# Two attention blocks in one kernel: B's diagonal key blocks packed in halves of 64 keys

## The chip, the cores and the metric

The kernel runs on one core of a Trainium2 chip. The time is device microseconds of one execution; of several executions the median is given. A core has five engines that run side by side, each with its own queue of instructions, worked off strictly in order: TensorE (PE in the profile; PEld is its weight loads), VectorE (DVE), ScalarE (ACT), GpSimd (POOL) and SyncE (SP, which here only issues transfers). They wait for each other through semaphores. Matmuls write into PSUM, here eight banks of 512 fp32 columns by 128 partitions; everything else lives in SBUF.

## The reference

Two independent attention blocks over 2048 rows of width 1024, 32 heads of 32, their outputs side by side.

```python
# A: plain attention over all 2048 keys
scores = jnp.einsum('bhqd,bhkd->bhqk', q, k) * Dh ** (-0.5)
p = _softmax(scores, axis=-1)
o = jnp.einsum('bhqk,bhkd->bhqd', p, v)          # then o @ wo
# B: four segments of 512 rows, causal inside a segment, with a running memory
for s in range(N):
    qs, ks, vs = (q[:, :, s].copy(), k[:, :, s].copy(), v[:, :, s].copy())
    logits = jnp.einsum('bhqd,bhkd->bhqk', qs, ks) * scale + mask   # mask: key after query
    p = _softmax(logits, axis=-1)
    a_dot = jnp.einsum('bhqk,bhkd->bhqd', p, vs)
    pq = phi(qs)
    num = jnp.einsum('bhld,bhde->bhle', pq, M)
    den = jnp.einsum('bhld,bhd->bhl', pq, z)[..., None] + 1e-06
    a_mem = num / den
    o = g * a_mem + (1.0 - g) * a_dot
    outs.append(o)
    pk = phi(ks)
    M = M + jnp.einsum('bhld,bhle->bhde', pk, vs)
    z = z + jnp.einsum('bhld->bhd', pk)
return o @ wo                                    # of the joined outs
```

## The kernel before

The program is not written out by hand: generator processes ask a planner (`Sched`, lines 172 to 370) for engines, banks and buffers, and the planner, while the kernel is built, simulates the engines with a cost for each operation and fixes the order of each queue. `Recorder` (lines 40 to 159) turns the data dependences of that order into semaphore waits, and `play` emits each engine's list. A dictionary `par` (line 398) holds the planner's settings: how far ahead of their use projections are due (`b`, `mem`, `ahead`), how many score slots must be left before PV work becomes urgent (`sl`, `pv`), at what rate B's units are mixed in among A's (`rate`) and so on.

Four heads make a group (128 partitions, 32 a head); each block has 8 groups. An **A unit** is one group by 256 queries (64 units); a **B unit** is one group in one segment of 512 queries and keys (32 units). For each the kernel works as follows.

Scores are computed transposed, keys on the partitions and queries on the columns. Four heads run side by side on the four row groups of TensorE (ROW mode), each writing its own bank. Six of the eight banks serve as three pairs for scores (`PAIRS`); banks 6 and 7 are shared by all other matmuls (`side`). `s_batch` (line 932) fills one step (u, k): for A, 256 queries against 256 keys for four heads, which takes two pairs; for B, k = 0 and 1 take two pairs, and k = 2 one pair. `parts` (line 914) lists what B's three steps hold, as (key tile, first query, width, first column): key tile 0 with all 512 queries; key tile 1 with the 384 from 128 on and, behind them, key tile 3 with its 128; key tile 2 with its 256. Each tile's first 128 columns are a diagonal block, half of which the causal mask throws away.

`exps` (line 988) turns a pair, 128x1024 scores, into probabilities: one exponential on ScalarE from PSUM to a slot of `PT` in SBUF (some of the first go to tiles not yet in use: WoB, OTA, OTB). For B, GpSimd then zeroes the masked triangle in place (`affine_select`, line 1011). The denominators need no maximum; a range check at the end raises a flag, and only if it is set a second, slower program runs (`shifted`, `emit` line 422).

`pv_unit` (line 1062) multiplies the probabilities by V and, for the denominators, by a block of ones, four heads on the four column groups (COL mode), into bank 6 or 7, and `finish` (line 1128) normalises on VectorE. A change between ROW and COL mode costs TensorE some time, so the planner runs COL work in stretches between score fills. COL work is also: projections (`proj`, line 685; `a_stream`, `b_proj`), the memory terms of B (`b_mem`, line 806; on VectorE it uses the buffer `mR` and, for the exponential of phi, a polynomial in `ze`, `ue`, `we` behind the lock `scr`), the output projections (`out_A`, `out_B`), and, where TensorE would be idle long, matmuls on zeros (`filler`).

At the end, every engine waits for the flag, loads it into a register and branches over the second program; SP then waits for all transfers (`drain`, line 143), channel by channel.

Of the kernel before, what the change touches and what calls it, by code (L numbers as in the profile page):

```python
# [39 lines left out]
class Recorder:  # L40
# [90 lines left out]
    def play(self, eng, name):  # L131
        for op in self.all:
            if op.ex != name:
                continue
            for d in op.waits:
                eng.wait_ge(self._sem_of(d), self.count[d])
            ins = op.fn(eng)
            if op.dma is not None:
                ins.then_inc(self.ch_sem[op.dma], 16)
            elif op.inc:  # L140
                ins.then_inc(self.sem[name], 1)

    def drain(self, eng):
        for c in range(self.NCH):
            if self.ch_n[c]:
                eng.wait_ge(self.ch_sem[c], 16 * self.ch_n[c])
# [226 lines left out]
def do(eng, fn, r=(), w=(), cost=0.1, prio=5, mode=None, tail=None, order=None, kb=None, hold=0.0, half=None):  # L373
    rq = Req()
    rq.half = half
    rq.order, rq.kb, rq.hold = order, kb, hold
    rq.eng, rq.fn, rq.r, rq.w, rq.cost, rq.prio, rq.mode = eng, fn, list(r), list(w), cost, prio, mode
    rq.tail = {"PE": 0.12, "ACT": 0.1, "DVE": 0.08, "POOL": 0.1, "SP": 2.0}[eng] if tail is None else tail
    return ("do", rq)
# [14 lines left out]
N256, N512 = 0.2235, 0.2175  # L394


class Kernel:
    par = dict(b=(16, 12, 9), mem=-4, memM=2, span=50, rate=0.58, ahead=20, sl=4, pv=10, ob=4, lead=6, b0=1, bpos=16, wob=40, mg=0.05, off=0, oks=(1,), sh=6, pd=4, o0=4, od=2, run=4, po=(1, 1), fp=2, fil=0.65, fs=0.15, ta=2, td=40, pvw=3, pvs=3, slk=0.12, pat=0.0, kh=3)
# [23 lines left out]
    def emit(self, block):  # L422
        def body(name):
            def f(eng):
                self.R.play(eng, name)
                self.R.after(eng, self.flagop)
                v = eng.value_load(self.flag[0:1, 0:1])
                with eng.If(v != 0):
# [4 lines left out]
                    if name == "SP":  # L433
                        self.R2.drain(eng)
                if name == "SP":
# [11 lines left out]
    def alloc(self):  # L447
# [16 lines left out]
        self.VB = [sb(f"VB{i}", [P, 4, 144]) for i in range(2)]  # L464
        self.PH = [sb(f"PH{i}", [P, 2, 512]) for i in range(2)]
# [8 lines left out]
        self.mR = sb("mR", [P, 512], F32)  # L474
# [13 lines left out]
        self.zero = sb("zero", [P, 32])  # L488
        self.maskbd = sb("maskbd", [P, P], F32)
        self.WoA = self.xA[:, :, :].rearrange("p i s -> p (i s)")[:, 0:NG * D].rearrange("p (j n) -> p j n", j=NG)  # L490
# [55 lines left out]
    def constants(self):  # L546
# [8 lines left out]
        for i in range(2):  # L555
            yield pool(lambda e, i=i: e.memset(self.VB[i][:, :, :], 1.0), [("VB", i)])
        yield pool(lambda e: e.memset(self.maskbd[:, :], 1.0), ["maskbd"])
# [124 lines left out]
    def pvprio(self):  # L682
        return 5 if len(self.slots.items) < self.par['sl'] or self.s_done else self.par['pv']
# [94 lines left out]
    def b_proj(self, n):  # L778
# [8 lines left out]
        for k in range(3):  # L787
# [7 lines left out]
            else:  # L795
                yield from self.proj(d, self.WB[k], ("WB", k), x, ["xB"], self.VT[n % 2][:, :], [("VT", n % 2)])
                yield self.turn(self.VB[b][:, :, 0:P], self.VT[n % 2][:, :], [("VT", n % 2)], [("VB", b)])
            if k == 1:
                Q.fire(("KQB", n))
            if k == 2:  # L800
                Q.fire(("VB", n))
            if n + 1 < 32:
                Q.spawn(self.load_WB(k, n + 1))
        Q.spawn(self.b_mem(n))

    def b_mem(self, n):
# [28 lines left out]
        if s > 0:  # L835
# [7 lines left out]
            def col(W, bank):  # L843
                def f(e):
                    for c in range(4):
# [5 lines left out]
            yield do("DVE", lambda e, bank=bank: e.transpose(self.mR[:, :], self.ps[:, bank, :]), r=[("ps", bank)], w=["mR"], cost=dve(512), prio=1)  # L851
            Q.give(self.side, [bank])
            yield do("DVE", lambda e: e.tensor_scalar(self.mr[:, :], self.mR[:, 0:512:32], 1e-6, None, ALU.add),
                     r=["mR"], w=["mr"], cost=0.1, prio=3)
            yield do("DVE", lambda e: e.reciprocal(self.mr[:, :], self.mr[:, :]), r=["mr"], w=["mr"], cost=0.2, prio=3)
            yield do("DVE", lambda e: e.transpose(self.mR[:, :].rearrange("p (a b) -> p a b", b=32), self.spread(self.mr[:, :])),
                     r=["mr"], w=["mR"], cost=dve(512), prio=3)
# [5 lines left out]
                     r=[("ps", bank), "mR", "gcol"], w=[("amem", b)], cost=dve(512) + 0.08, prio=1)  # L863
# [50 lines left out]
    def parts(self, u, k):  # L914
# [4 lines left out]
        return [[(0, 0, 512, 0)], [(1, 128, 384, 0), (3, 384, 128, 384)], [(2, 256, 256, 0)]][k]  # L919

    def s_all(self):
        Q = self.Q
        for u, k in self.order:
            yield from self.s_batch(u, k)
# [7 lines left out]
    def s_batch(self, u, k):  # L932
        Q = self.Q
        one = u[0] == "B" and k == 2
        parts = self.parts(u, k)
        if u[0] == "A":
            g = u[1]
            b = g % 2
            yield ("ev", ("KA", g, k))
            yield ("ev", ("QA", g, u[2]))  # L940
# [3 lines left out]
            keys = [("KA", b, k), ("QA", b, u[2])]  # L944
        else:
            b = u[1] % 2
            yield ("ev", ("KQB", u[1]))
            lhs = lambda t, hs: self.KQB[b][hs, 0, P * t:P * t + P]
            rhs = lambda q0, w, hs: self.KQB[b][hs, 1, q0:q0 + w]
            keys = [("KQB", b, 0), ("KQB", b, 1)]  # L950
        npair = 1 if one else 2
        slots = []
        for _ in range(npair):
# [4 lines left out]
        prs = yield acq(self.pairs, npair)  # L958
        mms = []
        if one:  # L960
            t, q0, w, _ = parts[0]
            for x in range(2):
                for h in (x, x + 2):
                    mms.append((prs[0][h // 2], x * 256, t, q0, w, h))
        else:
            for t, q0, w, col in parts:
                for h in range(4):
                    mms.append((prs[h // 2][h % 2], col, t, q0, w, h))

        def f(e, mms):  # L970
            for bk, col, t, q0, w, h in mms:
                hs = slice(32 * h, 32 * h + 32)
# [609 lines left out]
```

## Time and profile before

| what | us |
|---|---|
| median of 14 runs | 1115.26 (1113.3 to 1117.77) |
| the profiled execution | 1113.11 |
| its span | 1111.3 |
| TensorE matmuls (L973 scores, L1109 PV, L688 projections, L1197 and L1244 output) busy | 1044.9 |
| VectorE busy | 725.6 |
| GpSimd busy | 136.7, of it masks (L1011) 106.3 |
| granted TensorE clock, mean | 0.998 |

The profile is of one execution. A span begins with the first instruction and ends with the last. A busy time is the union of the instructions of an engine, so that overlapping ones count once; "mean ns of one" counts each from its own start to its own end, so in a closely packed queue the mean is longer than the distance from one to the next. A line number is that of the helper which recorded the instruction. "[0.25 <-PE ps L973]" behind a line of the timeline means that the engine was idle for 0.25 us before it, and that the last thing it waited for was TensorE's matmul of line 973. Transfers are 67.4 MB, 61 GB/s over the span, with the DMA engines mostly a quarter busy.

### The profile page before, as it was taken

To read this page: it belongs to the slowest core of one execution; us is meant where nothing else is said; L and a number is where in the kernel's file an instruction comes from. 1 tells how busy PE (TensorE), PEld (TensorE's weight loads), DVE (VectorE), ACT (ScalarE), POOL (GpSimd) and SP (SyncE) were. 2 spreads that over 40 slices of the span, in tenths; PEclk is the share of its full clock that TensorE was granted. 3 is DMA by queue.
4 is the path that set the end of the run, shared out by engine and by line. 5 is a ranking of instruction groups with operands and counts; after the bars stand their busy time and mean duration, and the time that the engine had idled before them with its cause. 6 is when DMAs were issued, how large, how long until landed. Compare 5 with 4: busy or idle time off the path is not lost.

```text
span 1111.3 us, 52489 instructions
## 1 busy us (share of the span) xinstructions
PE 1044.9 (94%) x24445; PEld 539.1 (49%) x24445; DVE 725.6 (65%) x1472; ACT 1089.9 (98%) x1189; POOL 136.7 (12%) x287
## 2 busy tenths in 40 slices
PE   8999999999899999989999999998999999999997
PEld 4545454444454444444445454444544444455554
DVE  2257566646675888888676788877557577664333
ACT  6999999999999999999999999999999999999996
POOL 1011111100201212121110211201111111110000
PEclk9999999999999999999999999999999999999999
DMA  9543331352121233132212232241222223201111
GB/s 191 102 110 80 61 73 41 55 93 50 36 50 36 59 61 66 42 78 55 60 40 56 47 62 61 49 84 45 41 58 42 45 45 60 88 18 36 41 41 66
DMA packets 213763, 67.40 MB, mean 61 GB/s; under 512 B 202786, under 2 KB 210978, under 8 KB 213538
## 3 DMA queue, kind: packets, MB, share of 16 engines
q1 hardware_dynamic: 212066, 63.07, 26.9%
q8 instruction: 192, 3.15, 1.2%
q10 hardware_dynamic: 1472, 0.92, 0.3%
q14 instruction: 33, 0.27, 0.1%
HBM read 36.70 MB, written 8.39 MB: 41 GB/s over the span
## 4 chain that ended last, share of the span: by engine, by line
ACT 88%; PE 9%; DVE 1%; DMA 1%; POOL 1%; issue 0%
ACT PT L1002 87%; PE ps L688 3%; PE ps L1109 2%; PE ps L973 2%; PE ps L1197 1%; DMA PKt<-PH 1%; ACT OTA L1002 1%; POOL PT L1011 0%; ACT OTB L1002 0%; PE ps L569 0%; DVE xA L625 0%; DVE KA L693 0%; PE ps L1244 0%; DVE PH L1039 0%; DVE PH L831 0%
## 5 line engine op out<-in xcount | busy, mean ns | idle before, releaser
L1002 ACT ACTIVATE PT<-ps 128x1024 bf16<-128x1024 f32 x1164 | 1068.4, 1267 | 2.7 <-PE ps L973 2.5
L1109 PE MATMUL ps<-PT,ones 128*32 128x256 bf16 (+1 forms) x4784 | 284.3, 271 | 0.9 <-issue 0.9
L1109 PE MATMUL ps<-PT,VA 128*32 128x256 bf16 x4016 | 241.4, 274 | 6.1 <-ACT PT L1002 5.0
L973 PE MATMUL ps<-QA,KA 32*128 32x256 bf16 x4096 | 203.6, 273 | 31.0 <-ACT PT L1002 25.7
L688 PE MATMUL ps<-xB,WB 128*32 128x512 bf16 (+1 forms) x3332 | 206.0, 365 | 2.6 <-DVE OD L1150 1.0
L688 PE MATMUL ps<-xA,WA 128*32 128x512 bf16 (+1 forms) x3476 | 205.2, 356 | 1.3 <-DVE xA L625 0.6
L1011 POOL TENSOR_SCALAR_AFFINE_SELECT PT<-PT 128x256 bf16<-128x256 bf16 (+1 forms) x224 | 106.3, 482 | 814.1 <-ACT PT L1002 808.8
L973 PEld LDWEIGHTS ps<-QA,KA 32*128 32x128 bf16 x4096 | 60.9, 92 | 194.5 <-ACT PT L1002 185.1
L1109 PEld LDWEIGHTS ps<-PT,ones 128*32 128x32 bf16 x4784 | 128.0, 97 | 32.8 <-issue 16.3
L1109 PEld LDWEIGHTS ps<-PT,VA 128*32 128x32 bf16 x4016 | 106.9, 96 | 45.3 <-issue 17.2
L688 PEld LDWEIGHTS ps<-xA,WA 128*32 128x32 bf16 x3476 | 80.2, 96 | 78.8 <-issue 28.0
L688 PEld LDWEIGHTS ps<-xB,WB 128*32 128x32 bf16 x3332 | 77.2, 96 | 78.9 <-issue 32.3
L1150 DVE COPY OD<-ps 128x512 f32<-128x512 f32 x127 | 86.6, 682 | 43.9 <-PE ps L1109 42.9
L1202 DVE CAST outsb<-ps 128x512 bf16<-128x512 f32 x55 | 37.8, 688 | 73.7 <-PE ps L1197 73.7
L693 DVE CAST KQB<-ps 128x512 bf16<-128x512 f32 x64 | 44.0, 688 | 61.5 <-PE ps L688 61.5
L693 DVE CAST VT<-ps 128x512 bf16<-128x512 f32 x64 | 44.0, 688 | 60.6 <-PE ps L688 57.5
L1197 PE MATMUL ps<-WoB,OTB 128*32 128x512 bf16 (+1 forms) x1100 | 68.2, 366 | 0.6 <-DVE OD L1150 0.6
L1156 DVE STREAM_TRANSPOSE OD<-Rall 128x256 f32<-128x256 f32 x127 | 56.0, 441 | 3.2
L1153 DVE STREAM_TRANSPOSE Dt<-OD 128x256 f32<-128x256 f32 x127 | 55.5, 437 | 2.9
L1197 PE MATMUL ps<-xA,OTA 128*32 128x512 bf16 (+1 forms) x888 | 53.4, 367 | 0.3 <-DVE KQB L693 0.3
L1109 PE MATMUL ps<-PT,VB 128*32 128x256 bf16 (+1 forms) x768 | 44.3, 259 | 7.2 <-POOL PT L1011 3.1
L973 PE MATMUL ps<-KQB 32*128 32x128 bf16 (+3 forms) x512 | 43.3, 302 | 6.5 <-ACT PT L1002 4.9
(95 smaller groups left out, 690.1 us busy)
## 6 DMA issues: line engine op xcount, KB each, us to landing
WB<-in_B_wk_dram SPq DMA_DIRECT2D x32, 256.0 KB, 3.0
WB<-in_B_wq_dram SPq DMA_DIRECT2D x32, 256.0 KB, 3.0
WB<-in_B_wv_dram SPq DMA_DIRECT2D x32, 256.0 KB, 3.2
out_dram<-outsb SPq DMA_DIRECT2D x63, 128.0 KB, 1.9
WA<-in_A_wqkv_dram SPq DMA_DIRECT2D x23, 256.0 KB, 3.3
WoB<-in_B_wo_dram SPq DMA_DIRECT2D x1, 2048.0 KB, 9.9
xA<-in_A_wo_dram SPq DMA_DIRECT2D x1, 2048.0 KB, 8.4
OTA<-in_A_x_dram SPq DMA_DIRECT2D x2, 256.0 KB, 5.1
```

The source lines that it names most:

```text
L688: ins = e.matmul(self.ps[32 * c:32 * c + 32, bank, lo:hi], W[:, i, 32 * c:32 * c + 32], x(i)[:, lo:hi], start=st, stop=sp)
L693: return e.tensor_copy(dst, self.ps[:, bank, 0:n])
L973: ins = e.matmul(self.ps[:, bk, col:col + w], lhs(t, hs), rhs(q0, w, hs), start=True, stop=True)
L1002: yield do("ACT", lambda e: e.activation(ap, self.ps[:, pr[0]:pr[1] + 1, :], ACTF.Exp, scale=sc), r=[("ps", bk) for bk in pr], w=keys, cos ...
L1011: yield do("POOL", lambda e, m=m, n=n: e.affine_select(m, m, pattern=[[0, n], [1, P]], compare_op=ALU.is_ge, fill=0.0, base=0, channel_mul ...
L1109: ins = e.matmul(out, l, r, start=st, stop=sp)
L1150: yield do("DVE", lambda e: e.tensor_copy(OD[:, :], self.ps[:, OB, :]), r=[("ps", OB)], w=[("OD", x), ("Rb", x)], cost=dve(2 * QU), prio=0 ...
L1153: yield do("DVE", lambda e: e.transpose(Dt[:, :], Rb), r=[("Rb", x)], w=[("Dt", x)], cost=dve(QU), prio=self.par["fp"], hold=0.15)
L1156: yield do("DVE", lambda e: e.transpose(Rb.rearrange("p (a b) -> p a b", b=32), self.spread(Rc)), r=[("Rc", ui % 64)], w=[("Rb", x)], cost ...
L1197: ins = e.matmul(self.ps[32 * c:32 * c + 32, bank, lo:hi], lhs(j)[:, 32 * c:32 * c + 32], W(j)[:, lo:hi], start=st, stop=sp)
L1202: return f(self.outsb[ob][:, :], self.ps[:, bank, :])
```

## The change

B's key tiles are cut into a low half (64 keys) and a high half. In a diagonal block of 128 keys by 128 queries the high keys' first 64 queries are masked entirely. So for the tile's first 64 queries only the low keys count, and the columns thus free on the upper 64 partitions take the high keys with 64 further queries: two half tiles share 64 score columns. On TensorE this is done by adding two matmuls into the same columns: one with weights K of the low keys, zero in the upper half ("lo"), one with the other half zero ("hi"). `KZ` holds the zero-padded K, copied by GpSimd for each unit (`b_k`); `VZ` the zero-padded V (`b_v`), and `half1` ones in one half, for PV. B's five exponentials a unit become four of 128x1024 and one of 128x512 (k = 2, 128 columns a head), with masks for each half.

The score loop now takes items of one pair each, A's and B's, two at a time (`s_all`, `s_batch`); a unit's short item is put so that it comes first of its two. With it in the step, the fill is three recorded pieces: the short item's heads 0 and 2, the other item, the short item's heads 1 and 3. Further: `mR` becomes a view of `ze`, under the lock `scr`; every GpSimd operation is made to depend on the one before (`Q7`); the branch at the end is written out with a branch hint, placed a number of operations before each engine's end; `drain` waits for the transfers in the order of issue; and the settings `par` differ.

```diff
-    def play(self, eng, name):
+    def play(self, eng, name, hint=0):
+        ops = [op for op in self.all if op.ex == name]
+        loc = None
+        for i, op in enumerate(ops):
+            if hint and i == max(0, len(ops) - hint):
+                loc = eng.mark_branch_hint_location()
...
+    if eng == "POOL":
+        rq.w.append("Q7")
...
+HINT = {"PE": 99999, "ACT": 300, "DVE": 700, "POOL": 999, "SP": 999}
-    par = dict(b=(16, 12, 9), mem=-4, memM=2, span=50, rate=0.58, ahead=20, sl=4, pv=10, ob=4, lead=6, b0=1, bpos=16, wob=40, mg=0.05, off=0, oks=(1,), sh=6, pd=4, o0=4, od=2, run=4, po=(1, 1), fp=2, fil=0.65, fs=0.15, ta=2, td=40, pvw=3, pvs=3, slk=0.12, pat=0.0, kh=3)
+    par = dict(b=(14, 10, 3), mem=-2, memM=10, span=50, rate=0.6, ahead=28, sl=5, pv=12, ob=3, lead=5, b0=1, bpos=20, wob=40, mg=0.05, off=0, oks=(1,), sh=3, pd=6, o0=4, od=0, run=4, po=(1, 1), fp=0, fil=0.65, fs=0.15, ta=1, td=10, pvw=3, pvs=3, slk=-0.05, pat=0.0, kh=3, pe=5, tk=(0.5, 1))
...
-                with eng.If(v != 0):
+                again, over = f"again_{name}", f"over_{name}"
+                eng.br_eq(v, 0, on_true=over, on_false=again).branch_hint(loc)
+                with self.nc.body(again, valid_engines=[eng.engine]):
...
+        yield pool(lambda e: e.memset(self.half1[:, :, :], 0.0), ["half1"])
+        yield pool(lambda e: e.memset(self.half1[0:H, 0, :], 1.0), ["half1"])
+        yield pool(lambda e: e.memset(self.half1[H:P, 1, :], 1.0), ["half1"])
+        yield pool(lambda e: e.memset(self.VZ[:, :, :], 0.0), ["VZ"])
+        yield pool(lambda e: e.memset(self.KZ[:, :, :], 0.0), ["KZ"])
...
     def pvprio(self):
-        return 5 if len(self.slots.items) < self.par['sl'] or self.s_done else self.par['pv']
+        if self.s_done:
+            return self.par["pe"]
+        return 5 if len(self.slots.items) < self.par['sl'] else self.par['pv']
...
+    def b_k(self, n):
+        if n:
+            yield ("ev", ("sB", n - 1))
+        b, H = n % 2, P // 2
+        src = self.KQB[b][:, 0, :].rearrange("p (t k) -> p t k", k=P)[:, :, 0:H]
+        yield do("POOL", lambda e: e.tensor_copy(self.KZ[:, :, 0:H], src), r=[("KQB", b, 0)], w=["KZ"], cost=0.35, prio=1)
+        self.Q.fire(("KZ", n))
+    def b_v(self, n):
+        if n:
+            yield ("ev", ("pvB", n - 1))
+        V, H = self.VB[n % 2], P // 2
+        for j in range(2):
+            yield do("POOL", lambda e, j=j: e.tensor_copy(self.VZ[H * j:H * j + H, j:4:2, :], V[0:H, j:4:2, 0:P]), r=[("VB", n % 2)], w=["VZ"],
+                     cost=0.4, prio=1)
+        self.Q.fire(("VZ", n))
...
-        return [[(0, 0, 512, 0)], [(1, 128, 384, 0), (3, 384, 128, 384)], [(2, 256, 256, 0)]][k]
+        H = P // 2
+        return [[("lo", 0, H, 0), ("hi", 1, H, 0), (0, H, 512 - H, H)], [(1, P + H, 5 * H, 0), (2, 2 * P + H, 3 * H, 5 * H)],
+                [("lo", 2, H, 0), ("hi", 3, H, 0), (3, 3 * P + H, H, H)]][k]
...
+            long = [(u, 0, 0), (u, 0, 1), (u, 1, 0), (u, 1, 1)]
+            j = 1 if len(items) % 2 else 4
+            items += long[:j] + [(u, 2, 0)] + long[j:]
...
+        if one[0]:
+            ops = [(st[0][:3], banks[0], 0.1, None), (st[1], banks[1], N256, None), (st[0][3:], banks[0], 0.1, True)]
         else:
...
+            n = 2 * P if one else 512
+            to = bass.AP(tensor=ap.tensor, offset=ap.offset, ap=[list(ap.ap[0]), [n, 2], [1, n]])
+            yield do("ACT", lambda e: e.activation(to, self.ps[:, pr[0]:pr[1] + 1, 0:n], ACTF.Exp, scale=sc),
+                     r=[("ps", bk) for bk in pr], w=keys, cost=0.483 if one else 0.91, prio=0)
...
             if k == 2:
-                ms = [(bass.AP(tensor=ap.tensor, offset=ap.offset, ap=[list(ap.ap[0]), [256, 4], [1, P]]), 4)]
+                ms = [(0, 0, 2 * H, 4), (H, 0, H, 8)]
             else:
-                ms = [(ap[:, :, c:c + P], 2) for c in ((0,), (0, 384))[k]]
+                ms = [(lo, col, 512, 2) for lo, col in (((0, 0), (H, 0), (H, H)), ((H, 0), (H, 5 * H)))[k]]
...
-                yield from self.pv_unit(u, [(0, [(0, 0, 256, 0)]), (1, [(1, 128, 128, 0)])], 0)
-                yield from self.pv_unit(u, [(0, [(0, 0, 256, 256)]), (1, [(1, 0, 256, 128), (3, 128, 128, 384)]),
-                                            (2, [(2, 0, 256, 0)])], 1)
+                H = P // 2
+                yield from self.pv_unit(u, [(0, [(0, H, 3 * H, H), ("lo", 0, H, 0), ("hi", P, H, 0)]), (1, [(1, 3 * H, H, 0)])], 0)
+                yield from self.pv_unit(u, [(0, [(0, 0, QU, QU)]), (1, [(1, 0, QU, H), (2, H, 3 * H, 5 * H)]),
+                                            (2, [("lo", 0, H, 0), ("hi", P, H, 0), (3, 3 * H, H, H)])], 1)
+                self.Q.fire(("pvB", u[1]))
```

The scores that ScalarE exponentiates are 1152 columns a head and B unit (512 + 512 + 128) instead of 1280.

## The prediction

> **What bounds the kernel now.** I read the page's engine table and groups first, then ScalarE's own order of time, TensorE around one B unit, and the last 11 us. The groups and the time order of ScalarE (columns of the second fence: start us, length us, engine, line, what, and the idle time before with its releaser):
>
> ```profile
> PE 1044.9 (94%) x24445; PEld 539.1 (49%) x24445; DVE 725.6 (65%) x1472; ACT 1089.9 (98%) x1189; POOL 136.7 (12%) x287
> ...
> L1002 ACT ACTIVATE PT<-ps 128x1024 bf16<-128x1024 f32 x1164 | 1068.4, 1267 | 2.7 <-PE ps L973 2.5
> ```
> ```profile
> 9.80 1.94 ACT L1002 ACTIVATE WoB<-ps 128x1024 bf16<-128x1024 f32 x2 [6.03 <-PE ps L973]
> ...
> 74.14 1.02 ACT L1002 ACTIVATE PT<-ps 128x1024 bf16<-128x1024 f32 x1 [0.25 <-PE ps L973]
> 75.35 645.71 ACT L1002 ACTIVATE PT<-ps 128x1024 bf16<-128x1024 f32 x704 [0.19 <-PE ps L973]
> ...
> 1101.18 0.58 ACT L1202 CAST outsb<-ps 128x512 bf16<-128x512 f32 x1 [1.05 <-PE ps L1197]
> ```
>
> ScalarE runs 1184 exponentials (1164 into PT, 20 more into borrowed tiles), all 128x1024: 1024 for A, and 5 for each of B's 32 units. One stretch holds 704 of them without a gap: 645.71/704 = 0.917 us each. From the first at 9.8 us to about 1100.1 us ScalarE is idle some 3 us. So the middle is ScalarE's, nothing else, and time is saved there only by giving it fewer columns. The ends are separate: 9.8 us ahead of the first exponential, 11.2 us after the last.
>
> **The exponentials: minus 13.9 us.** B's five become four of 128x1024 and one of 128x512 (four heads by 128 columns, where four by 256 stood). No exponential of that size is in the trace. One 1024-wide alone takes 1.02 us (at 74.14), the 512-wide cast from the same bank 0.585 us, so 512 columns are worth 0.435 us, and a short one in a queue costs 0.917 - 0.435 = 0.48 us. Bounds: half of the pitch, 0.459 (saves 14.7 in all), and the lone cast's 0.585 (saves 10.6). I take 0.48, the difference between like measurements: 32 x 0.435 = 13.9 us. Nothing hides ScalarE, so all of this is on the path.
>
> **The fill of the short pair: plus 2.6 us.** Each step of the changed loop takes two bank pairs, and where a short item comes first it is written in three TensorE pieces, the third waiting for the first. Now the short item takes one pair, so it can be filled earlier. Two places show it, one without and one with trouble:
>
> ```profile
> 72.12 0.28 PE L973 MATMUL ps<-KQB 32*128 32x256 bf16 x2
> ...
> 73.47 0.41 PE L874 MATMUL ps<-VB,PKt 128*32 128x129 bf16 x16 [0.85 <-DMA PKt<-PH]
> ...
> 73.81 0.28 PE L973 MATMUL ps<-KQB 32*128 32x256 bf16 x2
> ```
> ```profile
> 542.44 0.28 PE L973 MATMUL ps<-KQB 32*128 32x256 bf16 x2
> ...
> 542.99 0.28 PE L973 MATMUL ps<-KQB 32*128 32x256 bf16 x2
> ```
>
> Undisturbed, the halves start 0.55 us apart; at 73 us other work stood between, waited 0.85 us for a transfer, and the exponential at 74.14 came 0.25 us late. An ordinary fill (eight matmuls at 78.35) is modelled done at 78.75, and the exponential that needs it is due about 79.02 (75.35 + 4 x 0.917): a margin of 0.27 us. In the new order the short pair is done about 0.55 + 0.28 = 0.83 us after its start instead of 0.40. That is 0.43 late against 0.27, some 0.16 us of idle; its pieces are 64 columns wide instead of 256, which takes back up to 2 x 0.08 us (128 columns show 0.21 to 0.23 where 256 show 0.28). So 0 to 0.16 us, of which I take the middle, 0.08 x 32 = 2.6 us; ends 0 and 5.1. Behind the waiting third piece stands all of TensorE's PV and projection work; there the loss is absorbed by TensorE's slack, which I work out next. The two pairs are asked for when ScalarE starts a long exponential, since the short item is always first of its step: the cover stays 0.917 us. Were it the short one, 0.44 us of cover would be missing, 14 us over the kernel.
>
> **TensorE's other work: zero.** In units of four matmuls side by side, 256 columns start 0.109 us apart and 512 columns 0.217 (24 loads and matmuls in 1.52 us with the switch): PV 251 + 7, projections and output 444, memory 15, and 592 score fills at 0.32 plus 0.11 ahead, 255: 972 us against ScalarE's 1090. Scores and PV keep their columns in B (1280 per head each); they are cut in more pieces. Lower bound nothing; upper: twelve 64-column PV groups a unit priced like 128-column ones (0.054 in place of 0.027), 0.32 us, and 0.2 us for the X half of a mixed step, which runs on two row groups of four, and for narrow scores: 0.52 x 32 = 17 us. 989 against 1076 still leaves 87. I take 3 us and charge nothing, since ScalarE covers it; without that cover it would cost those 3 to 17 us. The last 100 us before the last exponential hold 2332 matmuls where 2230 is usual, with ScalarE still fully busy.
>
> [...]
>
> ```profile
> 78.34 0.12 PEld L973 LDWEIGHTS ps<-QA,KA 32*128 32x128 bf16 x8 [0.42 <-ACT PT L1002]
> 78.35 0.40 PE L973 MATMUL ps<-QA,KA 32*128 32x256 bf16 x8
> 78.67 0.98 PEld L688 LDWEIGHTS ps<-xA,WA 128*32 128x32 bf16 x24 [0.21 <-issue]
> ```
>
> Eight loads on alternating row groups take 0.12 us together, so I go by the row.
>
> **GpSimd and VectorE: zero.** Masks go from 7 a unit to 12, and three copies are added (KZ, and VZ in two). From 0.448 us for 256 elements a partition and 0.683 for 512: 0.21 + 0.92 ns per element. Ten masks of 128 elements at 0.33, one of 256 and one of 512: 4.4 us, where 3.4 stood. The copies, not in the trace, lie between 0.20 us (the memset of ident) and 0.65 (Zb); I take 0.45 as a mask of that size: 1.3 us. Every GpSimd operation now also waits for the one before; the one such wait visible (L550 on L549) cost 0.23, in a run of four masks none shows: 0 to 3.4 us a unit. Together 5.7 to 9.2 us a unit, in 34 us of the whole per unit; what hides it is the distance to PV: the last mask of the unit at 70 us ended at 75.86, and the PV that uses it ran after 80.5. Behind a waiting PV on TensorE stand the next score fills. A V copy that waits for its transpose (2.4 us from issue to landing) keeps the masks queued behind it waiting too. The mR buffer goes; its 24 chains now share the scratch of the exponential polynomial on VectorE, idle 35% of the time. SP loses no transfer; the first loads for B start at step 20 instead of 16, which leaves 12 steps (of two exponentials, 22 us) to B's first scores at step 32, where the transposed load of xB takes 8.8 us. The extra memsets at the start run on GpSimd while the first transfers land, well before 9.35 us.
>
> **The end: minus 2.0 us.** Queue entries of the branch and of the last waits (ns min/median/max, start us):
>
> ```profile
> L428 PEldq COMPARE_BRANCH  x1: 4653/4653/4653, 1106.3 to 1106.3; - x1
> ...
> L428 SPq COMPARE_BRANCH  x1: 53/53/53, 1106.4 to 1106.4; - x1
> ...
> L146 SPq EVENT_SEMAPHORE  x12: 17/28/28, 1109.9 to 1110.6; - x12
> ```
>
> TensorE's branch over the unused second program takes 4.65 us; SP's own lasts 0.05, but its next instruction comes 3.4 us later. The last output leaves at 1106.12 and lands in 1.9, so about 1108.0. If the hint lets the branch target be there in time, the span ends some 0.5 to 0.9 us after that, 1108.6 in place of 1111.3: a gain up to 2.7; if it does nothing, 0. I take 2.0, nearer the upper end since five engines are hinted. The work between the last exponential and 1106 is rearranged (ta 2 to 1, td 40 to 10); one output row is 8 x 0.217 = 1.7 us of TensorE, so plus or minus 1.7, taken as 0.
>
> **The sum.** Span 1111.3 - 13.9 + 2.6 - 2.0 = 1098.0; the profiled execution took 1113.11, 1.8 more than its span, so 1099.8. The median of the 14 runs, 1115.26, lies 2.15 above it: **1102 us**. By the bounds: -14.7 - 2.7 - 1.7 = -19.1 gives 1096, and -10.6 + 5.1 + 1.7 = -3.8 gives 1111.5; not all go wrong together, so its own range is 1097 to 1108.
>
> **Rivals.** First, the short pair is late oftener: planned other work lies between its pieces, as at 73 us. At 0.25 us a unit, as there, 8.0 in place of 2.6, and with no gain at the end: 1102 + 5.4 + 2.0 = 1109. For it: the wait exists today. Against: only six waits, 2.5 us, after the start.
>
> Second, slower: GpSimd becomes late for B's PV. At 9.2 us a unit against 4.15 us of its exponentials (4 x 0.917 + 0.48), the last mask is 5 us behind, where about 5 us are free; TensorE then stands in order at PV and the next score fill is late. ScalarE bears about 0.27 + 0.92 = 1.2 us of this. TensorE held 1.9 us a unit costs 0.7 x 32 = 22 us: 1124. It decides from 1.6 us of holding (0.4 x 32 = 13 us and more). For it: TensorE already waits 22 times on a mask (11.8 us). Against: GpSimd is 12% busy and most waits of its own are for ScalarE.
>
> Third, the short exponential costs what the long does (a fixed cost per bank): saving nothing, 1115.3 + 2.6 - 2.0, about 1116. Against: the cast's 0.585.
>
> **How the numbers follow.** A change under 0.2% (2.2 us) can't be told from none. Forecast 0.77, first rival 0.11 (most of it faster still, 0.03 within the bound), second 0.10, third 0.02. Faster 0.77 + 0.08 = 0.85; same 0.03 + 0.02 = 0.05; slower 0.10. The range 1096 to 1110 takes in the forecast and most of the first rival.
>
> **What would show it.** The group of exponentials near 1152 long ones at 0.917 and 32 short ones near 0.48; ScalarE's waits on L973's successor under 9 us after the start (above that, the first rival); waits of TensorE on the masks under 30 us (above 50, the second); TensorE's branch under 2 us. It would be wrong if ScalarE no longer were idle-free between 20 and 1080 us.

## The result, and the profile after

| | before | after |
|---|---|---|
| median of runs | 1114.7 us (47 runs) | 1120.03 us (10 runs, 1117.52 to 1123.82) |
| span of the profiled execution | 1111.3 | 1119.1 |
| first exponential starts | 9.8 | 10.7 |
| ScalarE's idle time between exponentials | 4.9 | 28.6 |
| end of the last exponential to end of span | 11.2 | 8.1 |

The ratio of after to before is 1.0047, 95% interval 1.0037 to 1.0058: slower, where 1102 us was forecast. The idle time is worked out from the trace, as the sum of what the ends of two successive exponentials lie further apart than 0.917 us for a long one and 0.487 for a short one (gaps under 25 ns left out).

The engine table and the costliest groups of the page of after, and from the groups by shape the short exponentials and the shortest masks (L1091 are the exponentials, L1103 the masks, L847 the V copies):

```profile
PE 1039.3 (93%) x25789; PEld 552.0 (49%) x25789; DVE 739.0 (66%) x1472; ACT 1083.3 (97%) x1188; POOL 228.5 (20%) x548
...
L1091 ACT ACTIVATE PT<-ps 128x1024 bf16<-128x1024 f32 x1164 | 1062.3, 1108 | 18.7 <-PE ps L1060 16.8
...
L847 POOL COPY VZ<-VB 64x256 bf16<-64x256 bf16 x64 | 32.6, 509 | 258.1 <-DMA VB<-VT 244.2
```
```profile
L1103 POOL TENSOR_SCALAR_AFFINE_SELECT PT<-PT 64x128 bf16<-64x128 bf16 x320 | 107.7, 336 | 348.6 <-ACT PT L1091 323.0
...
L1091 ACT ACTIVATE PT<-ps 128x512 bf16<-128x512 f32 x32 | 22.6, 706 | 0.9 <-PE ps L1060 0.9
```

ScalarE has less to do and waits more: before, its PT group idled 2.7 us, now 18.7, nearly all of it for score fills (L1060). GpSimd's busy time went from 136.7 to 228.5 us, and one new line idles 244.2 us for a transfer: the copy of V into its zero-padded form stands at the head of GpSimd's queue and waits for V's transpose.

What TensorE waited for, first its weight loads (PEld), then its matmuls (PE), of after; the columns are us in total, times, longest. The two sorts of row largely tell of the same stretches; the prediction's 11.8 us of before adds them (8.7 and 3.1):

```profile
PEld ps L1208 <- POOL PT L1103: 15.0, 19, 1.9
...
PEld ps L1208 <- POOL VZ L847: 11.0, 8, 2.3
```
```profile
PE ps L1208 <- POOL PT L1103: 10.2, 14, 1.6
PE ps L1208 <- POOL VZ L847: 7.8, 7, 2.0
```

So PV (L1208) waits for GpSimd three times as long as before: 26.0 us by the weight loads against 8.7, and by the prediction's sum, with smaller rows of other lines, 25.6 on masks and 19.7 on V copies. One such place in the order of time (start, length, engine, line, what, idle time before):

```profile
935.90 1.20 SPq L722 DMA_TRANSPOSE VB<-VT  x1
...
939.99 0.39 POOL L847 COPY VZ<-VB 64x256 bf16<-64x256 bf16 x1 [15.13 <-DMA VB<-VT]
...
940.51 4.05 POOL L1103 TENSOR_SCALAR_AFFINE_SELECT PT<-PT 64x128 bf16<-64x128 bf16 x10
...
944.62 0.39 POOL L847 COPY VZ<-VB 64x256 bf16<-64x256 bf16 x1
...
945.07 0.35 PE L1208 MATMUL ps<-PT,VB 128*32 128x192 bf16 x4 [2.04 <-POOL VZ L847]
...
947.11 0.61 PE L1060 MATMUL ps<-QA,KA 32*128 32x256 bf16 x8
...
947.77 1.94 ACT L1091 ACTIVATE PT<-ps 128x1024 bf16<-128x1024 f32 x2 [2.75 <-PE ps L1060]
```

Read downwards: the transpose issued at 935.90 is in at 939.9. Until then GpSimd stands at the first V copy, and the unit's masks, some ready to run by then, stand behind it. Ten masks of 64x128 then run without a pause; the second V copy is behind them. TensorE, in its written order, stands at PV until that copy is out, and the next score fill is queued behind PV. ScalarE idles 2.75 us.

The balance of the span: 32 x 0.43 = 13.8 us of exponentials saved, 23.7 more idle time, 0.9 later start, 3.1 shorter end: -13.8 + 23.7 + 0.9 - 3.1 = +7.7, where the spans differ by 7.8.

### The profile page after: what moved, and what is told of

It is laid out like the page before. It is cut to its first block, busy times and chain, and to the rows that moved or that the text cites. A ratio compares the mean times of both kernels' runs of the same rounds, so it can differ in the third digit from the quotient of the medians.

```text
span 1119.1 us, 55640 instructions
## 1 busy us (share of the span) xinstructions
PE 1039.3 (93%) x25789; PEld 552.0 (49%) x25789; DVE 739.0 (66%) x1472; ACT 1083.3 (97%) x1188; POOL 228.5 (20%) x548
## 4 chain that ended last, share of the span: by engine, by line
ACT 51%; PE 26%; DVE 13%; POOL 6%; issue 2%; DMA 1%; POOLq 0%; DVEq 0%
ACT PT L1091 50%; PE ps L711 11%; PE ps L1208 7%; POOL PT L1103 5%; PE ps L1060 5%; PE ps L1297 2%; DVE OD L1250 2%; DVE we L1129 1%; DVE OD L1256 1%; DVE Dt L1253 1%; DVE we L1130 1%; DVE VT L716 1%; DMA PKt<-PH 1%; DVE ze L869 1%; DVE ue L1126 1%
## 5 line engine op out<-in xcount | busy, mean ns | idle before, releaser
L1091 ACT ACTIVATE PT<-ps 128x1024 bf16<-128x1024 f32 x1164 | 1062.3, 1108 | 18.7 <-PE ps L1060 16.8
L1208 PE MATMUL ps<-PT,ones 128*32 128x256 bf16 (+2 forms) x4784 | 282.6, 268 | 0.0
L1208 PE MATMUL ps<-PT,VA 128*32 128x256 bf16 x4016 | 240.5, 274 | 5.0 <-ACT PT L1091 2.1
L1060 PE MATMUL ps<-QA,KA 32*128 32x256 bf16 x4096 | 210.2, 273 | 24.9 <-ACT PT L1091 21.6
L1103 POOL TENSOR_SCALAR_AFFINE_SELECT PT<-PT 64x128 bf16<-64x128 bf16 (+2 forms) x384 | 142.8, 372 | 355.5 <-ACT PT L1091 323.9
L1060 PEld LDWEIGHTS ps<-QA,KA 32*128 32x128 bf16 x4096 | 62.4, 92 | 172.9 <-ACT PT L1091 146.2
L1208 PEld LDWEIGHTS ps<-PT,ones 128*32 128x32 bf16 x4784 | 127.7, 97 | 30.8 <-issue 15.8
L1208 PEld LDWEIGHTS ps<-PT,VA 128*32 128x32 bf16 x4016 | 107.1, 96 | 41.5 <-issue 19.2
L847 POOL COPY VZ<-VB 64x256 bf16<-64x256 bf16 x64 | 32.6, 509 | 258.1 <-DMA VB<-VT 244.2
L1208 PE MATMUL ps<-PT,VB 128*32 128x192 bf16 (+2 forms) x768 | 45.1, 242 | 21.1 <-POOL PT L1103 10.2
```

The lines of the kernel that those rows point to most:

```text
L847: yield do("POOL", lambda e, j=j: e.tensor_copy(self.VZ[H * j:H * j + H, j:4:2, :], V[0:H, j:4:2, 0:P]), r=[("VB", n % 2)], w=["VZ"], cost ...
L1060: ins = e.matmul(out, l, r, start=a, stop=z)
L1091: yield do("ACT", lambda e: e.activation(to, self.ps[:, pr[0]:pr[1] + 1, 0:n], ACTF.Exp, scale=sc), r=[("ps", bk) for bk in pr], w=keys, c ...
L1103: yield do("POOL", lambda e, m=m, c=c: e.affine_select(m, m, pattern=[[0, c], [1, H]], compare_op=ALU.is_ge, fill=0.0, base=0, channel_mul ...
L1208: ins = e.matmul(out, l, r, start=st, stop=sp)
```

## The experiments

Each is one kernel; ratios are to the kernel before, run on the same chip, with 95% intervals. "Idle" and "tail" are worked out like the last two rows of the table above, from the one execution that was profiled; it lies up to 2.5 us from the median (vz_free: 1113.32 against 1115.83).

| kernel | median us | ratio | idle | tail |
|---|---|---|---|---|
| tail_alone | 1113.41 | 0.9984 (0.9974 to 0.9994) | 5.4 | 11.1 |
| pe_hint_off | 1122.64 | 1.0070 (1.0053 to 1.0087) | 27.7 | 10.2 |
| vz_free | 1115.83 | 1.0013 (1.0003 to 1.0024) | 21.0 | 8.1 |
| masks_free | 1106.35 | 0.9930 (0.9909 to 0.9951) | 14.0 | 8.1 |
| pool_free | 1106.78 | 0.9932 (0.9915 to 0.9948) | 14.7 | 8.1 |
| before_newset | 1127.27 | 1.0114 (1.0097 to 1.0131) | 16.8 | 11.5 |
| after_oldset | 1120.54 | 1.0056 (1.0039 to 1.0072) | 23.2 | 12.8 |
| copies_dve | 1103.05 | 0.9890 (0.9874 to 0.9907) | 12.8 | 8.1 |
| copies_dve_5 | 1103.07 | 0.9887 (0.9865 to 0.9909) | 11.4 | 8.1 |
| settings_only | 1106.64 | 0.9928 (0.9908 to 0.9948) | 13.8 | 8.1 |
| copies_only | 1138.76 | 1.0202 (1.0177 to 1.0226) | 45.4 | 10.9 |
| copies_actorder | 1111.61 | 0.9966 (0.9955 to 0.9977) | 17.7 | 10.5 |
| v_due9 | 1129.54 | 1.0117 (1.0098 to 1.0137) | 36.0 | 10.7 |
| mask18 | 1132.05 | 1.0147 (1.0130 to 1.0163) | 39.4 | 8.3 |
| settings12 | 1110.17 | 0.9948 (0.9932 to 0.9964) | 18.1 | 8.1 |

### The end of the program: tail_alone, pe_hint_off

tail_alone is the kernel before with the written-out branch, the hints and the drain in order of issue. pe_hint_off is the changed kernel, every queue in the same order, without TensorE's hint:

```diff
-HINT = {"PE": 99999, "ACT": 300, "DVE": 700, "POOL": 999, "SP": 999}
+HINT = {"PE": 0, "ACT": 300, "DVE": 700, "POOL": 999, "SP": 999}
```

> The kernel before, with only the branch hint, the written-out branch and the new order of the final waits. All theories take the end to be worth about 3 us, as the two traces show it (TensorE's branch 4.65 to 0.49 us): 1111.5 to 1112.5, if the hint costs nothing elsewhere. If the hint, which stands at TensorE's first instruction, disturbs its instruction supply (the third theory), TensorE's idle times of over 0.35 us that end by nothing but issue rise from 15 (9 us) to over 25 (over 15 us), and the time is 1114 or more.

> The changed kernel without TensorE's hint, all else and the order of every queue the same. Theory 1 (GpSimd late for B's PV) and theory 2 (fill and order of the short item): the waits of ScalarE stay near 24 us, the end gets its 4 us back, 1123 to 1125. Theory 3 (the hint disturbs TensorE's supply): issue gaps over 0.35 us fall from 36 to about 15, ScalarE's waits fall by 6 us or more, the time is 1119 or less in spite of the longer end.

TensorE's branch (its queue entry, ns min/median/max, then the start in us) of after, of tail_alone and of pe_hint_off:

```profile
L437 PEldq COMPARE_BRANCH  x1: 491/491/491, 1117.1 to 1117.1; - x1
```
```profile
L435 PEldq COMPARE_BRANCH  x1: 4617/4617/4617, 1107.4 to 1107.4; - x1
```
```profile
L437 PEldq COMPARE_BRANCH  x1: 3755/3755/3755, 1116.6 to 1116.6; - x1
```

In the changed program the hint takes TensorE's branch from 3.76 to 0.49 us, and without it the tail is 2.1 us longer. In the program of before the same hint, at the same place (TensorE's first instruction), leaves 4.62 where 4.65 stood. So the hint doesn't cause the loss, and whether it helps depends on the program: with the hint TensorE's branch takes 0.40 to 0.50 us in after and ten other profiles here, but 4.62 in tail_alone, 4.49 in copies_only and 4.33 in v_due9; in these the span ends 0.3 to 0.4 us after it, as it does in the kernel before. On what this depends, the runs don't tell, nor what TensorE's branch waits for where it takes 3.76 to 4.65 us. tail_alone, at 1113.41, missed the expected 1111.5 to 1112.5: it gained 1.6 us in the median, but its profiled tail is only 0.05 us shorter, so where that came from stays open.

### The same order, with parts of GpSimd's work taken out: vz_free, masks_free, pool_free

These keep the order of every queue of the changed kernel, and change only what an instruction does. In vz_free each V copy becomes a memset of two columns that doesn't wait for the transpose, so the zero-padded V of B's diagonal blocks is left out. In masks_free each mask touches two columns, so most of B's causal mask is left out, and the V copies are whole. pool_free has both.

```diff
-            yield do("POOL", lambda e, j=j: e.tensor_copy(self.VZ[H * j:H * j + H, j:4:2, :], V[0:H, j:4:2, 0:P]), r=[("VB", n % 2)], w=["VZ"],
-                     cost=0.4, prio=1)
+            fn = lambda e, j=j: e.memset(self.VZ[H * j:H * j + H, j, 0:2], 0.0)
...
-                yield do("POOL", lambda e, m=m, c=c: e.affine_select(m, m, pattern=[[0, c], [1, H]], compare_op=ALU.is_ge,
+                yield do("POOL", lambda e, m=m, c=c: e.affine_select(m, m, pattern=[[0, 1], [1, 2]], compare_op=ALU.is_ge,
```

> The changed kernel, same order of every queue, with the two V copies per unit cut to a memset of two columns that does not wait for V's transpose (VZ stays zero, so these keys are left out of B's output). Theory 1, in the form that the V copy stands ahead of the masks and waits for the transfer: TensorE's waits on the copy (19 us) vanish and those on masks (25 us) shrink by half or more, ScalarE's idle falls by 6 to 10 us, time 1110 to 1114. If the masks themselves are too many, only the 19 us go and the time falls by 3 to 5. Theories 2 and 3: within 2 us of the changed kernel.

> The changed kernel, every queue in the same order, the masks cut to two columns each (B's causal mask is left out almost wholly), the V copies whole and waiting for the transpose as in the change. With both cut the kernel was 13 us faster than the changed one, with the copies alone cut 4. If masks and copies add up, 1110 to 1112; if each is the other's cover (a copy late for PV whether or not masks stand between its two halves), 1114 or more; if the masks behind the waiting copy are the whole matter, 1108 or less.

> As the run before, and the masks cut to two columns each (B's causal mask is left out almost wholly): GpSimd does next to nothing, same order of every queue. This is all that theory 1 can claim: ScalarE's idle after the start falls from 24 us to 10 to 13, time 1106 to 1110. Theory 2 expects the 4 us of idle just behind the 32 short exponentials to stay here too. Theories 2 and 3 alone: 1118 or more.

masks_free, the masks' group by shape and then TensorE's waits on GpSimd:

```profile
L1103 POOL TENSOR_SCALAR_AFFINE_SELECT PT<-PT 64x2 bf16<-64x2 bf16 x384 | 85.9, 224 | 371.0 <-ACT PT L1091 347.9
L847 POOL COPY VZ<-VB 64x256 bf16<-64x256 bf16 x64 | 32.2, 503 | 280.5 <-DMA VB<-VT 263.5 <-PE ps L1208 14.3
```
```profile
PEld ps L1208 <- POOL VZ L847: 2.9, 6, 1.3
PEld ps L1208 <- POOL PT L1103: 2.7, 5, 0.9
```

With masks of 224 ns instead of 336 (and 437, 661 for the longer forms), GpSimd is busy 58 us less, TensorE's waits on it nearly vanish, on V copies too, and ScalarE's idle time falls by 14.6 us. The V copies still wait for transfers as long as in after (263.5 us): that wait alone does little harm. In medians masks_free is 13.7 us below after; by the ratios, (1.0047 - 0.9930) x 1115 = 13.0.

Freeing the V copies alone brings 4.2 us in the medians and leaves PV's waits on masks where they were (27.7 us by the sum, after 25.6). With both parts out nothing more is gained than with the masks. So it is the length of GpSimd's whole queue that holds PV; the waiting copy adds to it and isn't the main part. In this order of work GpSimd costs the changed kernel some 13 us. TensorE's waits on VectorE, 32.2 us before and 60.6 in after, stay at 62.8 in masks_free, so the 13 us are not theirs.

### Is it the settings? before_newset, after_oldset

The dictionary `par` of each kernel is put into the other (`pe` and `tk`, which the old kernel doesn't use, stay with after).

> The kernel before with the planner settings of the change. If the settings themselves, and not the packing, lose the time (V due 3 steps ahead instead of 9, a shorter slack before scores), this kernel is slower than before by 5 us or more. If they are bad only together with the copies and masks that the change adds, it is within 4 us of before, 1111 to 1119.

> The changed kernel with the settings of before (V due 9 steps ahead of its unit). If the late V is the lever, TensorE's waits on the V copy fall from 19 us to under 6 and the time is 1108 to 1114. If the planner's costs for GpSimd are (a mask is put at 0.23 us, measured 0.34), PV still stands behind late masks: waits on masks over 20 us, 1116 or more.

The new settings make the old kernel slower by 12.7 us over its 1114.5 or so, far more than expected of settings alone. With the old ones the changed kernel comes to the same 1120.5 by another way: ScalarE idles 5.4 us less, and the tail is 4.7 longer; the waits on V copies fall from 19.7 to 7.8 us, but those on masks stay (29.1, after 25.6), as the second reading expected. In both kernels the new settings go with more waits of TensorE on VectorE: 63.7 us where 32.2 stood in the old one, 60.6 where after_oldset has 40.6 in the changed one, while the old kernel's waits on masks hardly move (13.5, before 11.8). That these waits cost the 12.7 us wasn't tested. So the planner's settings are worth as much as the change's whole saving, and a setting that suits one kernel's work doesn't suit the other's.

### A version that beats both: copies_dve, and which part of it does

copies_dve is the changed kernel with the three copies on VectorE, V's projection due 9 steps before its use instead of 3, masks planned 0.06 us dearer, and other settings moved with them:

```diff
+MC = 0.18
-    par = dict(b=(14, 10, 3), mem=-2, memM=10, span=50, rate=0.6, ahead=28, sl=5, pv=12, ob=3, lead=5, b0=1, bpos=20, wob=40, mg=0.05, off=0, oks=(1,), sh=3, pd=6, o0=4, od=0, run=4, po=(1, 1), fp=0, fil=0.65, fs=0.15, ta=1, td=10, pvw=3, pvs=3, slk=-0.05, pat=0.0, kh=3, pe=5, tk=(0.5, 1))
+    par = dict(b=(16, 12, 9), mem=0, memM=6, span=50, rate=0.59, ahead=32, sl=6, pv=10, ob=4, lead=5, b0=1, bpos=18, wob=40, mg=0.05, off=0, oks=(1,), sh=3, pd=6, o0=4, od=0, run=4, po=(1, 1), fp=2, fil=0.65, fs=0.15, ta=1, td=40, pvw=3, pvs=3, slk=0.12, pat=0.0, kh=3, pe=5, tk=(0.5, 1))
...
-            yield do("POOL", lambda e, j=j: e.tensor_copy(self.VZ[H * j:H * j + H, j:4:2, :], V[0:H, j:4:2, 0:P]), r=[("VB", n % 2)], w=["VZ"],
-                     cost=0.4, prio=1)
+            yield do("DVE", lambda e, j=j: e.tensor_copy(self.VZ[H * j:H * j + H, j:4:2, :], V[0:H, j:4:2, 0:P]), r=[("VB", n % 2)], w=["VZ"],
+                     cost=0.2, prio=1)
...
-                         r=keys, w=keys, cost=0.12 + 0.054 * c, prio=0)
+                         r=keys, w=keys, cost=MC + 0.054 * c, prio=0)
```

> The changed kernel with the three copies per unit on VectorE instead of GpSimd, V due 9 steps ahead, the mask's planned cost raised by 0.06 us, and settings to go with it. GpSimd then has masks and little else. Theory 1: TensorE's waits on GpSimd and the copies under 15 us, ScalarE's idle after the start 10 to 14 us, time 1104 to 1110, faster than both kernels. If fill and order of the short item lose most (theory 2), 1112 or more.

> copies_dve once more, beside the three on the same chip: 1101.5 to 1104.5, ratio to before 0.988 to 0.990.

1103.05 and 1103.07 us: some 12 us below the kernel before and 17 below the changed one. By shape and by wait, in copies_dve_5:

```profile
L1104 POOL TENSOR_SCALAR_AFFINE_SELECT PT<-PT 64x128 bf16<-64x128 bf16 x320 | 106.4, 332 | 733.9 <-ACT PT L1092 708.6
...
L848 DVE COPY VZ<-VB 64x256 bf16<-64x256 bf16 x64 | 13.8, 215 | 9.0 <-DMA VB<-VT 8.0
```
```profile
PEld ps L1209 <- POOL PT L1104: 8.2, 20, 1.3
```

The masks are as long as in after; now 708.6 us of GpSimd's idle time is for ScalarE, as in the kernel before (808.4), and PV's wait on masks, by the weight loads, is back at 8.2 us (8.7 before). Then the two parts by themselves: settings_only leaves the copies on GpSimd, copies_only moves them and keeps the plan's settings.

> The changed kernel with the settings of copies_dve (V due 9 steps ahead instead of 3, dearer planned masks, more slots in hand), the three copies left on GpSimd. Queue theory (what hurt was a copy on GpSimd that stands ahead of the masks; the copies must leave that engine): most of the 17 us stay lost: about 1113, TensorE's waits on masks over 22 us, on V copies still 8 or more. Rival, the plan (what hurt was that V's copy and the masks were planned with too little time; on whichever engine they are): about 1103 to 1106, waits on V copies under 4 us, masks 10 to 18, excess of ScalarE 12 to 15 us.

> The changed kernel with its own settings, the three copies moved to VectorE. Queue theory: 1104 to 1108, masks under 18 us. Rival, the plan: V is still due 3 steps ahead, so the wait for its transfer only goes to VectorE, where the normalising and the casts queue behind it: 1113 to 1120, TensorE's waits on VectorE above the 60.6 us of the changed kernel.

The plan decides the time. settings_only does just the work of the changed kernel on the same engines and takes 1106.64 us, 13.4 less. How it does so is only in part what the rival said: the waits on V copies are 2.7 us and ScalarE's idle time 13.8 (5.5 of it one gap at 592 us), as expected, but the waits on masks are 21.4, not 10 to 18. With these settings moving the copies gains another 3.6 us (copies_dve_5). With the old ones it loses: copies_only is the slowest of all, far above the rival's 1113 to 1120. TensorE's waits on VectorE are 87.0 us there (60.6 in after), those on masks still 23.2, and the branch at the end takes 4.49 us again, which makes the tail 2.8 longer. A stretch of VectorE in copies_only, and ScalarE behind it:

```profile
856.66 0.69 DVE L717 CAST KQB<-ps 128x512 bf16<-128x512 f32 x1
857.26 0.21 DVE L848 COPY VZ<-VB 64x256 bf16<-64x256 bf16 x1
857.39 0.21 DVE L839 COPY KZ<-KQB 128x256 bf16<-128x256 bf16 x1
857.53 0.68 DVE L718 TENSOR_SCALAR QA<-ps 128x512 bf16<-128x512 f32 x1
...
858.35 1.91 PE L712 MATMUL ps<-xB,WB 128*32 128x512 bf16 x32 [0.94 <-DVE QA L718]
...
860.31 0.69 DVE L717 CAST KQB<-ps 128x512 bf16<-128x512 f32 x1 [0.40 <-PE ps L712]
...
861.15 0.40 PE L892 MATMUL ps<-PH,Zb 128*32 128x512 bf16 x4 [0.54 <-DVE KQB L717]
...
862.44 6.52 ACT L1092 ACTIVATE PT<-ps 128x1024 bf16<-128x1024 f32 x7 [5.31 <-PE ps L1061]
```

VectorE works almost without a gap, and TensorE stands behind it twice in 3 us, 1.5 us together. The next score fill stands behind both waits and behind projections and PV in TensorE's written order, and ScalarE idles 5.31 us. So in this plan the copies on VectorE hold TensorE more than they did on GpSimd.

### The short exponential's cover: copies_actorder

In the changed kernel the planner often exponentiates the long item of a step first and the short one second, so that the next fill has 0.49 us of cover. copies_actorder makes the long one wait for the short one:

```diff
+        if after:
+            yield ("ev", after)
```

> copies_dve with ScalarE made to take the short exponential before the long one of its step in every unit. If the short one's cover of 0.49 us for the next fill costs the idle time just behind it (2.1 us in copies_dve, 3.8 in the changed kernel), this idle time falls under 1 us and the time by 1.5 to 2.5 us: 1101. Rival: the short pair, whose last piece is filled last, is then waited for itself, 0.1 to 0.4 us in up to 16 units: 1103 to 1108, the idle time moved to just ahead of the short ones.

In after the short one is second in 16 of 32 units, in copies_dve_5 in 10; each of these has idle time right behind it, and no other unit has. It goes from 3.8 us in after and 2.1 in copies_dve_5 to nothing, as expected, and on the short ones themselves it stays at 0.2 us: the rival's wait isn't there. The kernel is nevertheless 8.5 us slower than copies_dve_5: the added rule moves the rest of the plan, its longest gap is 3.8 us at 608 us, and the tail is 2.4 longer. That the order causes this idle time is confirmed; that taking it away gains the 1.5 to 2.5 us is not shown.

### One number of the plan at a time: v_due9, mask18, settings12

v_due9 has one setting changed, V due 9 steps ahead. mask18 has one planned cost changed, that of a mask. settings12 is settings_only with the old cost of a mask.

```diff
-    par = dict(b=(14, 10, 3), mem=-2,
+    par = dict(b=(14, 10, 9), mem=-2,
```

> The changed kernel with one setting changed: B's V projection is due 9 steps ahead of its use instead of 3; all else, the planned costs too, as in the changed kernel. If the V copy that waits for its transfer at the head of GpSimd's queue is what hurts: the waits on V copies fall from 19.7 us to under 5 and with them the masks' 25.6 to under 18; 1108 to 1113. If it is that GpSimd's work is planned too cheap: V waits fall, masks stay near 25 us: 1115 to 1118.

> The changed kernel with one number of the planner changed: a mask is planned 0.06 us dearer (0.18 + 0.054 for each block of 64 columns instead of 0.12 + 0.054; a short one measures 0.336, planned 0.228 before and 0.288 here). Work and settings are the same, the order is not. If masks planned too cheap are what hurts: masks' waits under 15 us, 1106 to 1111. If V's due time is: V waits stay above 12 us and the time within 4 us of 1120.

> The changed kernel with the settings of copies_dve, masks planned as cheap as in the changed kernel, copies on GpSimd: against settings_only (1106.64) it has the planned mask cost alone changed. If the settings do it: 1105 to 1109, masks 15 to 25 us. If the mask's planned cost did it: 1112 to 1118, masks above 25 us.

Both single changes did to GpSimd's waits part of what was expected (by the sum: v_due9 8.3 us on V copies and 31.7 on masks; mask18 10.7 and 21.8; after 19.7 and 25.6), and yet both kernels are slower than after, by 9.5 and 12 us, far from all that was expected. The loss turns up elsewhere: in mask18 TensorE waits 69.9 us for VectorE (after 60.6). In v_due9 the span is 10.1 us longer: 2.6 at the end, where the branch takes 4.33 us again, and 7.4 of idle time, nearly all of it right behind short exponentials (10.9 us, after 3.8; 3.7 of it one gap at 95 us behind a wait of TensorE). settings12, at 1110.17, lies between its two marks: the settings as a whole bring most of the gain, but the waits on masks are 27.0 us, as the other reading had it. The 3.5 us to settings_only are 2.2 by the ratios, whose intervals overlap, so what the planned mask cost is worth there isn't clear of noise. No single number repairs the plan, and which of the settings matter together is not settled.

## Why the prediction was wrong

**Exponentials, minus 13.9: right.** 1152 long (1132 of them into PT) and 32 short ones are left, and the short ones end 0.487 to 0.493 us after the one before where nothing is late (0.48 forecast). The third rival (they cost what long ones do) falls.

**Fill of the short pair, plus 2.6: near by luck.** It came to 4.9 us, 3.8 behind the short ones and 1.1 on them. The sum put 0.08 us on every short one, for its late third piece; 30 of the 32 weren't late at all, and two lost the 1.1. The rest comes from what the text ruled out: it held that the short item always comes first and the cover stays 0.917. It is filled first, but in half of the units ScalarE took it second. That cost 3.8/16 = 0.24 us each, where the text priced 0.44 on all 32, 14 us. The first rival's mark (ScalarE's waits on fills after the start under 9 us) was passed, 16.8 us, though mostly through the waits described next.

**The end, minus 2.0: close.** -3.1 in the span. TensorE's branch is 0.49 us, under the 2 foretold, and its hint is worth 2.1 of the 3.1 (pe_hint_off). That the hint took in this program was a chance the text allowed for, not a thing it knew: in tail_alone it didn't. Ahead of the first exponential 0.9 us were lost, which the sum had at nothing.

**"GpSimd and VectorE: zero": this step failed.** Its durations were right: masks of 128 elements 0.336 us (0.33 forecast), copies 0.446 and 0.509 (0.45 forecast). What failed is the cover. The "about 5 us" from the last mask to PV were read at one unit of the kernel before, and it is the one with the longest cover of all 32: taken for every unit from the same trace, the unit's last mask ends 0.06 to 5.1 us before the PV matmul that uses it, 2.9 in the median and under 1.6 in nine units. The change adds 91.8 us to GpSimd, 2.9 a unit, so the old trace itself spoke against zero. Besides, the planner sets that distance anew, from its own costs. It counts a short mask as 0.12 + 2 x 0.054 = 0.228 us, and it took 0.336. That is part of it at most: masks planned 0.06 us dearer go with 4 to 6 us less of waits on masks (25.6 to 21.8 in mask18, 27.0 to 21.4 from settings12 to settings_only), and mask18 was slower all the same. The text even named the queue that formed, "A V copy that waits for its transpose (2.4 us from issue to landing) keeps the masks queued behind it waiting too", and charged nothing for it. In this plan GpSimd costs some 13 us (masks_free).

**The second rival was right in its mechanism and too demanding in its marks.** It was to decide from 1.6 us of holding a unit, and to show by over 50 us of waits on masks. The masks alone show 25.6, under the 30 that stood for the forecast, because the V copies' 19.7 weren't counted with them; both together, 45.3, still miss the 50. By the weight loads TensorE is held 26.0/32 = 0.8 us a unit, and ScalarE loses 13/32 = 0.4: half of the holding arrives, where the rival took 0.7 of 1.9, some third. In its favour stood TensorE's 22 waits on masks in the old trace, which was the evidence to weigh more: that cover was already used up in places.

**What is left.** Against the forecast span of 1098.0, after is 21.1 us longer: 14.6 us of idle time that go with the masks' length, 2.3 from the short fill (3.8 + 1.1 - 2.6), -0.2 from the end and the start (-1.1 + 0.9), and some 4 in small waits of other kinds that masks_free has too. TensorE's waits on VectorE, which nearly doubled, may be behind these; no run tests it. Nothing speaks against the zero for TensorE's own work: it is busy 1039.3 us where 1044.9 stood.

**A term was missing: the plan.** The prediction treated the settings as part of the change that moves nothing but the tail and B's first loads. With the changed kernel's work on the same engines, other settings and planned costs gave 1106.6, 1110.2, 1120.0, 1120.5, 1129.5 and 1132.1 us; the old kernel gave 1114.7 and 1127.3. That is a spread of 25 us, nearly twice the saving, and the range of 1096 to 1110 had no room for it.

## What to carry to other kernels

When an order of work is generated, a change of the work is also a new order: the hiding place read in the old trace didn't carry over here, and the spread between plans (25 us) belongs in the range. A hiding place is read at all units, not at one (0.06 to 5.1 us here, where the one showed about 5). An engine that is busy 20% of the time can still cost the bottleneck time, as GpSimd some 13 us here, if another engine needs what comes out of its queue; count all of that queue's products that the reader waits for, not one kind. To separate work from order, first keep every queue as it is and shrink the suspected instructions, and only then re-plan.

## What the runs showed of the hardware

Some of TensorE's waits in after cost it a second time, through its clock. The granted clock (PEclk, the third column from the right) of after, behind the wait that ends at 945 us, around two waits of 0.79 and 0.76 us between 655 and 657, and in an undisturbed stretch:

```profile
946.00:949.00 3.00, 3.00 (x40) 0.87 (x36) 2.22 (x5) 1.23 (x2) 1.69 (x4) 0.58 0.00 0
656.00:662.00 6.00, 5.24 (x107) 2.15 (x111) 4.88 (x12) 4.38 (x6) 2.07 (x5) 0.72 0.02 4
400.00:410.00 10.00, 9.52 (x244) 5.15 (x232) 6.04 (x14) 10.00 (x12) 1.24 (x3) 1.00 0.26 57
```

After 2.04 us without a matmul, the 3 us from 946 on run at 0.58, and the fill of eight matmuls at 947.11 takes 0.61 us where those at 942.63 and 949.47 take 0.40. By the clock that is 0.42 x 3 = 1.3 us more of TensorE's time, an estimate; ScalarE's 2.75 us of idle time hold part of it. Not every wait does this: behind single ones of 1.61 us at 217 and 1.58 us at 534 the clock stays at 1.00. Over whole executions the mean is 0.998 before and in settings_only, 0.997 in after, 0.991 in v_due9 and mask18, and in copies_only:

```profile
core 0: 1138.6 us, clock 0.985
```

Worked out in the same way, 0.015 x 1138.6 = 17 us of TensorE's time go there, an estimate, the end of the span included. So by this estimate TensorE loses time on top of its waits in the slow plans; no run here keeps the clock up under such a plan, so what it costs ScalarE isn't shown. Nor is what decides whether the clock falls: in after the mean of the stretch fell behind a wait of 2.04 us, the longest of TensorE's, and around the two of 0.79 and 0.76 us (0.72 over 656 to 662), but not behind the ones of 1.61 and 1.58 us.
